# Splitting the load of token blocks 12 to 15 in two, and moving one output store on SyncE's queue, in a one-core attention-plus-MLP kernel

## The chip, the core and the metric

The kernel runs on one core of one Trainium2 chip. A core has five instruction streams that run side by side and wait for one another through semaphores: TensorE (PE, the matrix products, with its weight loads PEld), VectorE (DVE), ScalarE (ACT), GpSimd (POOL) and SyncE (SP), which here does nothing but issue DMA transfers. Each stream is worked off strictly in order. The metric is device time in microseconds of one launch.

## The reference

A token stream of 2048 x 640 (bfloat16) passes a pre-norm attention block with a compressive memory, and then a pre-norm MLP with SiLU. The sequence is cut into four segments of 512 tokens:

```python
for s in range(4):                                  # 32 heads of width 20
    qs, ks, vs = q[:, :, s], k[:, :, s], v[:, :, s]
    p = softmax(qs @ ks.T * 20 ** -0.5 + causal_mask)
    a_dot = p @ vs
    pq = phi(qs)                                    # phi(t) = t + 1 if t > 0 else exp(t)
    a_mem = (pq @ M) / (pq @ z + 1e-6)              # memory of the segments before
    outs.append(g * a_mem + (1 - g) * a_dot)        # g = sigmoid(beta)
    pk = phi(ks); M += pk.T @ vs; z += pk.sum(tokens)
h  = x + concat(outs) @ wo                          # q, k, v from layernorm(x)
h2 = h + silu(layernorm(h) @ w1) @ w2               # w1: 640 x 1728, w2: 1728 x 640
```

## The kernel before, in words

The 2048 tokens are 16 blocks of 128, four to a segment. All weights stay on the chip. The token blocks live in `x_tok`, a ring of 12 slots, so block 12 takes the slot of block 0, and so on to block 15 in the slot of block 3. A block is loaded, normalized, used as the residual of the attention output, normalized again, used as the residual of the MLP, and stored from the same slot.

Work is cut into tasks. The table `ORDER` lists all tasks in one hand-set order; each name goes to its engine's stream in the order of the table, and the number after a colon is a buffer slot. A tracker puts in the semaphore waits that the reads and writes need; DMA transfers have semaphores of their own, called lanes. So moving a name in `ORDER` moves an instruction in one engine's stream and changes what it stands behind. The names that matter here (the first digit is the segment, or the two digits the block):

- `x12` loads blocks 12 to 15 (L578, function `load_x`). Its slots are those of blocks 0 to 3, so it waits for the stores `out0` to `out3` (L1367), which share one lane, to land.
- `out0` stores output block 0 from `x_tok`; `o0` to `o3` (L1362, DVE) make the output blocks.
- `n1_st12` to `n1_st15` (L742, DVE) take the layer-norm statistics of the blocks of the last segment. On DVE they stand between steps `s1_...` of segment 1's MLP (L1322, writing `sT`), the first of them, `s1_1_0`, right behind `n1_st12`. A step `s1_f_0` also frees the PSUM bank in which the MLP product `h1_1_f_0` (L1307, PE) of that feature block stood, after `th1_f_0` (L1316, ACT) has read it.
- `vp1...` (L927, twelve small copies, function `pvirt`) copy pieces of `phiQ` into `phiQv`. A head is 20 wide and sits in 32 rows; the 12 spare rows of each hold pieces of further heads, the spare heads, and the copies bring their features to the front. Segment 1 has three memory products that read `phiQv`, and the first, in `tn13` (L1038, PE), waits for all twelve copies.
- `kt10`, `kt23` (L1207) are DMA transposes of key features; `n2_tr6`, `n2_tr7`, `n2_tr4`, `n2_tr5` (L798) are DMA transposes of the second layer norm's output of blocks 4 to 7 into `hT`, from a ring of four buffers `xn_rot`. The steps `n2_ap4` and `n2_ap5` (L769, DVE) write the two buffers that `n2_tr6` and `n2_tr7` have read, and so wait for these to land.

Of the kernel before, what the change touches and what calls it, by code (L numbers as in the profile page):

```python
# [324 lines left out]
D = 640  # L325
# [85 lines left out]
s0_1_1 qk18a0:2 e18a0:2 vt25/S av17:1 oe17/A:0 kt23:1 h2_2_0:6 h2_2_1 n2_ap6:1 n2_st5:6 n2_tr6:0 n2_r7/G mk18e_256
n2_ap7:3 n2_tr7 phb220 vt22/S e18a2 qk19b0:0 pha230:0 phb230 vp21/S:0 e19b0:4 tn17:4 nm17:3,1 n2_ap4:1 n2_tr4 pha200:0
h2_2_2 e19b2 h2_2_3 mk18a_0 n2_r5/G qk19a0:0 h2_3_0:4 h2_3_1 e19a2:0 o2 ad17:0 vp22/S e19a0 n2_ap5:3 n2_tr5 out2/S
mk19a_0 vp24/S ex200:0 kh14/D av18:6 oe18/D:0 vt210/A phb200 qk20b0:0 e20b+:3 h2_3_2 mk19b_0 h2_3_3 o3 vp25/S ex201:1
kg14/G mz12:7 mb10:0,0 tn18:1 nm18:3,0 mk19b_384 av19:0 h1_1_10_0:6 oe19/A:0 phb201 qk21b0:0 th1_10_0:1 tn16:4 ma12
# [40 lines left out]
h2_15_3_1 out15_0/A o15_1 h2_15_1_2 h2_15_2_2 h2_15_3_2 o15_2 out15_2/A out15_1/S fill2:2
""".split()


ONE_EXP = {row.partition("+")[0] for row in ORDER if row[0] == "e" and "+" in row}  # L460


def build(nc, es, A_x, A_wq, A_wk, A_wv, A_wo, A_beta, B_x, B_w1, B_w2, out):
    T = Tracker()
    pools = {
# [8 lines left out]
    G = Graph(pools)  # L474
# [950 lines left out]
```

## Time and profile before

| | |
|---|---|
| median of 3 runs | 298.25 us (298.09 to 298.98) |
| the profiled execution, its own time | 298.47 us |
| its span in the trace | 296.6 us |
| PE busy | 285.5 us |
| DVE, ACT, POOL busy | 222.1, 217.2, 140.0 us |
| granted TensorE clock | 1.0 |

The span runs from the first to the last instruction of the trace; the profiled execution's own time is 1.87 us more, for what lies around it. In rows of the trace the first number is the start in us from the span's beginning, the second the length, then the engine (SPq is SyncE's queue of DMA issues), the line, the operation, out<-in, a count, and in brackets how long the engine stood idle before it and who released it. A row for a DMA shows how long its issue took; when it landed is told by "DMA to landing", counted from the start of the issue. "issue" as the releaser means that the profile shows nothing that was waited for. A matmul row's end holds the time in which the last result drains, so the next row starts up to 0.2 us before that end.

### The profile page before, as it was taken

The page shows a single profiled execution, that of the slowest core. Times are in us where ns is not written, and L with a number is a line of the kernel's source. Part 1 is how long each engine was busy: PE and PEld are TensorE (multiplying, and loading weights), DVE is VectorE, ACT ScalarE, POOL GpSimd, SP SyncE. Part 2 cuts the span into 40 slices and gives each one's busy share as a digit, 9 for nine tenths or more (in the row PEclk, how much of TensorE's full clock was granted, in tenths as well). Part 3 has the DMA queues.
Part 4 walks back from the last instruction along what each step waited for, and adds up shares of the span by engine and source line. Part 5 has one row for each costly group of instructions (what it writes and reads, how often), then busy time and mean ns, then how long its engine had stood idle before and what let it go on. Part 6 is the DMA issues. An engine that isn't in the chain of part 4 may idle for free.

```text
span 296.6 us, 7437 instructions
## 1 busy us (share of the span) xinstructions
PE 285.5 (96%) x2991; PEld 168.3 (57%) x2991; DVE 222.1 (75%) x506; ACT 217.2 (73%) x266; POOL 140.0 (47%) x257
## 2 busy tenths in 40 slices
PE   8898889999999989999999999999999999999997
PEld 6775545545665445566643444465665457764575
DVE  3897899769979679899688967759967688626522
ACT  4985989999999888998879999788759751014400
POOL 6247836744655576646525656355576630200000
DMA  7958773804953321254452400144181023230002
GB/s 230 371 181 115 178 123 82 219 5 107 164 101 58 72 39 23 39 110 62 104 139 48 80 1 2 26 76 88 19 102 32 0 58 77 67 68 25 22 22 91
DMA packets 49906, 25.40 MB, mean 86 GB/s; under 512 B 39488, under 2 KB 48032, under 8 KB 49872
## 3 DMA queue, kind: packets, MB, share of 16 engines
q1 hardware_dynamic: 47788, 22.69, 36.5%
q10 hardware_dynamic: 2084, 2.23, 2.4%
q8 instruction: 24, 0.39, 0.6%
q14 instruction: 10, 0.08, 0.1%
HBM read 10.41 MB, written 2.62 MB: 44 GB/s over the span
## 4 chain that ended last, share of the span: by engine, by line
PE 80%; DVE 8%; DMA 4%; ACT 3%; POOL 2%; issue 2%; SPq 1%; DVEq 0%; ACTq 0%
PE ps_all L1349 19%; PE ps_all L1307 15%; PE ps_all L866 12%; PE ps_all L964 7%; PE ps_all L1272 7%; PE ps_all L827 5%; PE ps_all L1008 5%; ACT PT L976 2%; PE ps_all L619 2%; DMA x_tok<-in_A_x_dram 2%; PE ps_all L1092 2%; PE ps_all L1038 1%; PE ps_all L1225 1%; DMA w_sb<-w_sb 1%; POOL PT L987 1%
## 5 line engine op out<-in xcount | busy, mean ns | idle before, releaser
L976 ACT ACTIVATE PT<-ps_all 128x1024 bf16<-128x1024 f32 (+1 forms) x120 | 153.2, 1310 | 16.9 <-PE ps_all L964 15.7
L987 POOL TENSOR_SCALAR_AFFINE_SELECT PT<-PT 128x512 bf16<-128x512 bf16 x128 | 81.6, 648 | 59.6 <-ACT PT L976 57.5
L1349 PE MATMUL ps_all<-w_sb,sT 128*128 128x320 bf16 (+2 forms) x462 | 64.9, 295 | 0.0
L1307 PE MATMUL ps_all<-hT,w_sb 128*128 128x512 bf16 (+1 forms) x325 | 63.0, 337 | 0.6 <-DVE sT L1322 0.5
L1316 ACT ACTIVATE th<-ps_all 128x512 f32<-128x512 f32 (+2 forms) x70 | 34.1, 505 | 35.3 <-PE ps_all L1307 31.2
L1349 PEld LDWEIGHTS ps_all<-w_sb,sT 128*128 128x128 bf16 x462 | 43.2, 98 | 18.3 <-issue 1.8
L1322 DVE SCALAR_TENSOR_TENSOR sT<-th,ps_all 128x512 bf16<-128x512 f32 (+2 forms) x70 | 37.8, 560 | 16.9 <-ACT th L1316 16.0
L1307 PEld LDWEIGHTS ps_all<-hT,w_sb 128*128 128x128 bf16 x325 | 29.8, 98 | 26.0 <-issue 3.2
L763 POOL TENSOR_TENSOR rst<-rst,eps_c 128x1 f32<-128x1 f32 x32 | 18.3, 576 | 24.1 <-DVE rst L757 22.8
L742 DVE BATCH_NORM_STATS2 stt<-x_tok 128x6 f32<-128x320 bf16 x62 | 27.2, 481 | 2.6 <-DMA x_tok<-in_A_x_dram 2.2
L1362 DVE SCALAR_TENSOR_TENSOR x_tok<-ps_all,x_tok 128x640 bf16<-128x640 f32 (+3 forms) x18 | 13.3, 745 | 16.7 <-PE ps_all L1349 16.6
L1070 POOL TENSOR_TENSOR otok<-on 128x320 bf16<-128x320 bf16 x24 | 19.0, 797 | 11.4 <-DVE on L1062 11.4
L1272 PE MATMUL ps_all<-wo_sb,oT 128*128 128x320 bf16 x160 | 23.8, 299 | 0.0
L883 DVE CAST QK<-ps_all 128x512 bf16<-128x512 f32 x23 | 15.7, 688 | 8.8 <-PE ps_all L866 8.6
L1062 DVE TENSOR_TENSOR on<-ps_all,rd 128x640 bf16<-128x640 f32 x24 | 19.8, 825 | 0.9
L1272 PEld LDWEIGHTS ps_all<-wo_sb,oT 128*128 128x128 bf16 x160 | 15.0, 98 | 7.2 <-issue 1.8
L866 PE MATMUL ps_all<-xT,wkr 128*128 128x512 bf16 x75 | 18.7, 380 | 0.0
L827 PE MATMUL ps_all<-wv_sb,xT 128*128 128x320 bf16 x120 | 18.3, 299 | 0.3
L866 PE MATMUL ps_all<-xT,wqr 128*128 128x512 bf16 x75 | 18.2, 380 | 0.0
L1008 PE MATMUL ps_all<-PT,Vx 128*32 128x512 bf16 (+3 forms) x384 | 16.4, 301 | 0.1
L769 DVE TENSOR_SCALAR xn_rot<-x_tok,mvt,rst 128x640 bf16<-128x640 bf16 x32 | 15.0, 479 | 1.6 <-POOL rst L763 0.9
L842 DVE CAST Vx<-ps_all 128x640 bf16<-128x640 f32 x15 | 12.3, 818 | 5.2 <-PE ps_all L827 5.0
(106 smaller groups left out, 338.8 us busy)
## 6 DMA issues: line engine op xcount, KB each, us to landing
w_sb<-in_B_w_dram SPq DMA_DIRECT2D x5, 432.0 KB, 5.7
x_tok<-in_A_x_dram SPq DMA_DIRECT2D x3, 640.0 KB, 8.9
w_sb<-in_B_w_dram SPq DMA_DIRECT2D x3, 480.0 KB, 4.4
out_dram<-x_tok ACTq DMA_DIRECT2D x8, 160.0 KB, 1.8
out_dram<-x_tok SPq DMA_DIRECT2D x7, 160.0 KB, 2.0
QKV<-QK SPq DMA_DIRECT2D x12, 72.0 KB
wo_sb<-in_A_wo_dram SPq DMA_DIRECT2D x1, 800.0 KB, 10.0
w_sb<-in_B_w_dram SPq DMA_DIRECT2D x1, 640.0 KB, 4.3
```

What stands on the lines that cost most here:

```text
L742: T.add(DV, lambda e, hh=hh: e.bn_stats(out=stt[:, s, 6 * hh:6 * hh + 6], in_=xb[:, 320 * hh:320 * hh + 320]), reads=R((xa, xsub)), writes ...
L827: fns.append(lambda e, c=c, hh=hh: e.matmul(bank(ps, hh)[:, 0:320], lhsT=xT_[:, c, 128 * i:128 * i + 128], rhs=wv_sb[:, c, 320 * hh:320 * ...
L866: fns = [lambda e, kc=kc: e.matmul(bank(ps)[:, lo:hi], lhsT=wt[:, kc, c, :], rhs=xT_[:, kc, lo:hi], start=(kc == 0), stop=(kc == NC - 1)) ...
L964: fns.append(lambda e, j=j, o=o, r=r, q0=q0, q1=q1, qa=qa, ka=ka: e.matmul(ps_all[:, o:o + q1 - q0], lhsT=ka[32 * r:32 * r + DH, 128 * j:1 ...
L976: T.add(AC, lambda e: e.activation(out=pt[:, pta.slot, q0:q0 + nq, 0:width], in_=sc3[:, b0:b0 + nq, 0:width], func=ACT.Exp, scale=SCALE), ...
L987: T.add(PO, lambda e: e.affine_select(out=v, in_=v, pattern=[[0, 4], [1, 128]], compare_op=ALU.is_ge, fill=0.0, base=0, channel_multiplier ...
L1008: fns.append(lambda e, j=j, r=r, h=h, pa=pa, pt=pt, co=co, q0=q0, ji=ji: e.matmul(bank(po)[32 * r:32 * r + 32, q0:hi], lhsT=Vx[:, vx.slot, ...
L1272: fns.append(lambda e, c=c, hh=hh: e.matmul(bank(ps, hh)[:, 0:320], lhsT=oT[:, c, 128 * i:128 * i + 128], rhs=wo_sb[:, c, 320 * hh:320 * h ...
L1307: fns = [lambda e, c=c: e.matmul(bank(ps)[:, lo:hi], lhsT=w1_sb[:, c, 128 * f:128 * f + 128], rhs=hT[:, c, lo:hi], start=(c == 0), stop=(c ...
L1316: T.add(AC, lambda e: e.activation(out=th[:, tha.slot, lo:hi], in_=bank(ps)[:, lo:hi], func=ACT.Tanh, scale=0.5), reads=R((ps, [0])), writ ...
L1322: T.add(DV, lambda e: e.scalar_tensor_tensor(out=sT[:, f, lo:hi], in0=th[:, tha.slot, lo:hi], scalar=1.0, in1=bank(ps)[:, lo:hi], op0=ALU. ...
L1349: fns.append(lambda e, f=f, t0=t0, fr=fr, hh=hh, n=n: e.matmul(bank(pa, hh)[:, 0:n], lhsT=sT[:, f, t0:t0 + 128], rhs=w2_sb[:, fr, c0 + 320 ...
```

## The change

Two things move, and nothing that is computed changes.

1. The one load of blocks 12 to 15 (640 KB) becomes two of 320 KB, each with a lane of its own: `x12` for blocks 12 and 13 and `x14` for blocks 14 and 15. `x14` stands where `x12` stood, right behind `out3`. `x12` now stands much further ahead, behind the key transpose `kt23`, where of the lane of the stores only `out0` and `out1` are in front of it.
2. `out0` stood ahead of the transpose `kt10`, with seven of the twelve copies `vp1...` behind it; it now stands behind the last copy, `vp14`.

```diff
@@ ORDER
-ex231:2 tn11:6 nm11:0,1 pr200:4 qe200/A:0 mk12e_0 ex210:0 mk12e_256 qk14b0:0 av13:5 mzc7 oe13/D:1 out0/S mzc4 pha211:0
+ex231:2 tn11:6 nm11:0,1 pr200:4 qe200/A:0 mk12e_0 ex210:0 mk12e_256 qk14b0:0 av13:5 mzc7 oe13/D:1 mzc4 pha211:0
...
-th0_7_1:0 vp110/S vp12/S vp14/S tn13:6 nm13:2,1 ad13 pr201:5 qe201/A qk15a0:0 e15a2:4 e15a0 s0_7_1 tn10:6 nm10:2,0
+th0_7_1:0 vp110/S vp12/S vp14/S out0/S tn13:6 nm13:2,1 ad13 pr201:5 qe201/A qk15a0:0 e15a2:4 e15a0 s0_7_1 tn10:6
...
-s1_1_0 qk18a0:2 e18a0:2 vt25/S av17:1 oe17/A:0 kt23:1 h2_2_0:6 h2_2_1 n2_ap6:1 n2_st5:6 n2_tr6:0 n2_r7/G mk18e_256
+s0_1_1 qk18a0:2 e18a0:2 vt25/S av17:1 oe17/A:0 kt23:1 x12/S h2_2_0:6 h2_2_1 n2_ap6:1 n2_st5:6
...
-e20a+:2 out3/S x12/S n1_st12:6 n1_r12/G h1_1_1_0:4 th1_1_0:1 s1_1_0 vp210/S h1_1_12_0:7 th1_12_0:0 mk20b_0 n1_st13:0
+th1_7_0:1 th1_4_0:0 s1_7_0 s1_4_0 qk20a0:0 e20a+:2 out3/S x14/S n1_st12:6 n1_r12/G h1_1_1_0:4 th1_1_0:1 s1_1_0 vp210/S
...
@@ in build()
     for s in range(NSEG):
         if s == NSEG - 1:
-            load_x(12, 4, 8 * s + P["x3"])
+            load_x(12, 2, 8 * s + P["x3"])
+            load_x(14, 2, 8 * s + P["x3"])
         declare_front(s)
```

SyncE's queue around the copies of the spare heads' features, before: the row `out_dram<-x_tok` is `out0`, the `phiKt` row behind it `kt10`, the `phiQv` rows the copies, the two `hT` rows `n2_tr3` and `n2_tr2`.

```order
L927 DMA phiQv<-phiQ 12x1536
L1367 DMA out_dram<-x_tok 128x640
L1207 DMA_TRANSPOSE phiKt<-phiK 128x4x128
L927 DMA phiQv<-phiQ 8x1x512
L798 DMA_TRANSPOSE hT<-xn_rot 128x5x128
L927 DMA phiQv<-phiQ 8x1024
L798 DMA_TRANSPOSE hT<-xn_rot 128x5x128
L927 DMA phiQv<-phiQ 8x1024
L927 DMA phiQv<-phiQ 12x1536
L927 DMA phiQv<-phiQ 8x1024
L927 DMA phiQv<-phiQ 8x1x512
L927 DMA phiQv<-phiQ 8x1024
```

The same place in the changed kernel (all its lines below the table are one higher):

```order
L928 DMA phiQv<-phiQ 12x1536
L1208 DMA_TRANSPOSE phiKt<-phiK 128x4x128
L928 DMA phiQv<-phiQ 8x1x512
L799 DMA_TRANSPOSE hT<-xn_rot 128x5x128
L928 DMA phiQv<-phiQ 8x1024
L799 DMA_TRANSPOSE hT<-xn_rot 128x5x128
L928 DMA phiQv<-phiQ 8x1024
L928 DMA phiQv<-phiQ 12x1536
L928 DMA phiQv<-phiQ 8x1024
L928 DMA phiQv<-phiQ 8x1x512
L928 DMA phiQv<-phiQ 8x1024
L1368 DMA out_dram<-x_tok 128x640
```

Two transposes and seven copies that stood behind the store are now ahead of it.

SyncE's queue around the new place of `x12`, before: the `phiKt` row is `kt23`, the `hT` rows are `n2_tr6`, `n2_tr7`, `n2_tr4` and `n2_tr5`, the store is `out2`.

```order
L1207 DMA_TRANSPOSE phiKt<-phiK 128x4x128 [waits s_pool,s_dve]
L798 DMA_TRANSPOSE hT<-xn_rot 128x5x128 [waits s_pe,s_dve]
L798 DMA_TRANSPOSE hT<-xn_rot 128x5x128 [waits s_dve]
L914 DMA QKV<-QK 8x1x1024
L927 DMA phiQv<-phiQ 8x1024 [waits s_dve]
L798 DMA_TRANSPOSE hT<-xn_rot 128x5x128 [waits s_dve]
L927 DMA phiQv<-phiQ 8x1x512
L798 DMA_TRANSPOSE hT<-xn_rot 128x5x128 [waits s_dve]
L1367 DMA out_dram<-x_tok 128x640
```

And in the changed kernel:

```order
L1208 DMA_TRANSPOSE phiKt<-phiK 128x4x128 [waits s_pool,s_dve]
L579 DMA x_tok<-in_A_x_dram 128x2x640 [waits l_out0]
L799 DMA_TRANSPOSE hT<-xn_rot 128x5x128 [waits s_pe,s_dve]
L799 DMA_TRANSPOSE hT<-xn_rot 128x5x128 [waits s_dve]
L915 DMA QKV<-QK 8x1x1024
L928 DMA phiQv<-phiQ 8x1024 [waits s_dve]
L799 DMA_TRANSPOSE hT<-xn_rot 128x5x128 [waits s_dve]
L928 DMA phiQv<-phiQ 8x1x512
L799 DMA_TRANSPOSE hT<-xn_rot 128x5x128 [waits s_dve]
L1368 DMA out_dram<-x_tok 128x640
```

One more DMA, with a wait on the stores' lane, stands ahead of the four transposes. The streams of PE, ACT and POOL hold the same instructions in the same order as before; on DVE the only difference is a wait of `n1_st15` on the new lane of `x14`.

More of the change, by code (lines that the diff above doesn't have):

```diff
@@ L411 @@
[L411 to L415, printed above, removed]
@@ L456 @@
[L456 removed]
+th0_7_1:0 vp110/S vp12/S vp14/S out0/S tn13:6 nm13:2,1 ad13 pr201:5 qe201/A qk15a0:0 e15a2:4 e15a0 s0_7_1 tn10:6
+nm10:2,0 mk15a_0 pha201:2 pr221:5 av14:4 oe14/A:1 qe221/D av12:7 oe12/D:0 qk15b0:0 mb11:0,0 kg11/G tn14:4 nm14:1,1
+pr241:6 qe241/D:0 e15b+:0 mk15b_0 h1_0_12_1:7 th0_12_1:1 s0_12_1 kt14:0 vt26/S:0 ad14 mk15b_384 qk16b0:0 e16b0:2
+tn12:4 nm12:2,1 h1_0_4_1:6 th0_4_1:0 vt20/S s0_4_1 ad10 h1_0_10_1:7 e16b2 h1_0_0_1:0 th0_10_1:1 av15:1 ad12 th0_0_1:0
@@ new lines @@
+s0_0_1 s0_10_1 oe15/A:1 mk16b_0 mk16b_384 qk16a0:2 e16a2:4 h1_0_6_1:6 pha220:0 e16a0 tn15:0 nm15:1,0 pr240:7 qe240/D
+ex211:1 th0_6_1:1 s0_6_1 h1_0_5_1:4 ad15 th0_5_1:0 s0_5_1 qk16e0:0 mk16a_0 e16e0:5 ot6:0 ot7 e16e2 mk16e_0 pha210:0
+ot4 pr230:5 pha240:0 phb210 qe230/D v22:6 ve22/D ex230:0 ot5 out1/S h1_0_13_1:4 th0_13_1:0 qk17b0:0 e17b2:3
+h1_0_11_1:5 th0_11_1:1 vt29/S pha231:1 phb231 phb211 e17b0 wo6:6 mk16e_256 s0_13_1 s0_11_1 qk18b0:2 e18b2:6 mk17b_0
+e18b0 mk18b_0 rs6 n2_st6:3 ex220:2 av16:0 oe16/D:1 wo7:6 rs7 n2_r6/D qk17a0:2 wo4:0 vt28/S e17a+:0 h1_0_9_1:7
@@ new lines @@
+th0_9_1:0 ex240:1 kg10/G vt27/S n2_st7:0 mk18b_384 vt21/S mk17b_384 vt211/S h1_0_3_1:6 mk17a_0 rs4 th0_3_1:1 n2_st4:2
+s0_9_1 qk18e0:2 e18e0:1 n2_r4/D wo5:0 s0_3_1 vt23/S h1_0_2_1:7 e18e2 mk18e_0 phb240 rs5 th0_2_1:0 s0_2_1 h1_0_1_1:6
+th0_1_1:1 vt24/S s0_1_1 qk18a0:2 e18a0:2 vt25/S av17:1 oe17/A:0 kt23:1 x12/S h2_2_0:6 h2_2_1 n2_ap6:1 n2_st5:6
+n2_tr6:0 n2_r7/G mk18e_256 n2_ap7:3 n2_tr7 phb220 vt22/S e18a2 qk19b0:0 pha230:0 phb230 vp21/S:0 e19b0:4 tn17:4
+nm17:3,1 n2_ap4:1 n2_tr4 pha200:0 h2_2_2 e19b2 h2_2_3 mk18a_0 n2_r5/G qk19a0:0 h2_3_0:4 h2_3_1 e19a2:0 o2 ad17:0
@@ new lines @@
+vp22/S e19a0 n2_ap5:3 n2_tr5 out2/S mk19a_0 vp24/S ex200:0 kh14/D av18:6 oe18/D:0 vt210/A phb200 qk20b0:0 e20b+:3
+h2_3_2 mk19b_0 h2_3_3 o3 vp25/S ex201:1 kg14/G mz12:7 mb10:0,0 tn18:1 nm18:3,0 mk19b_384 av19:0 h1_1_10_0:6 oe19/A:0
+phb201 qk21b0:0 th1_10_0:1 tn16:4 ma12 s1_10_0:0 nm16:0,1 e21b+:4 mk21b_0 mk21b_384 h1_1_7_0:7 h1_1_4_0:6 ad18
+th1_7_0:1 th1_4_0:0 s1_7_0 s1_4_0 qk20a0:0 e20a+:2 out3/S x14/S n1_st12:6 n1_r12/G h1_1_1_0:4 th1_1_0:1 s1_1_0 vp210/S
+h1_1_12_0:7 th1_12_0:0 mk20b_0 n1_st13:0 n1_r13/G mk20b_384 vp28/S qk20e0:0 h1_1_11_0:5 n1_ap12:3 e20e+:0 h1_1_8_0:4
@@ new lines @@
+qk21a0:0 s1_12_0 th1_11_0:1 h1_1_5_0:6 e21a+:5 th1_5_0:0 n1_st15:5 mk21a_0 n1_ap13:2 mk20a_0 s1_11_0 s1_5_0 mk20e_0
+mk20e_256 h1_1_2_0:7 th1_2_0:1 s1_2_0 vp20/S qk22a0:0 e22a0:6 kt20:0 vp211/S kg20/G:0 n1_st14:4 vp26/S th1_8_0:1
+kg23/D n1_r14/D h1_1_6_0:5 th1_6_0:0 vp29/S n1_tr12:0 v30:6 n1_r15/D s1_6_0 e22a2 h1_1_0_0:0 n1_ap14:0 s1_8_0
+n1_ap15:3 mk22a_0 kh23/G av21:1 ve30/A:1 mb12:0,0,0,0 av20:2 qk22b0:3 vp23/S th1_0_0:0 s1_0_0 n1_tr13 mz20:7 ma20
+oe21/A:1 e22b+:1 mk22b_0 vp27/S tn21:0 h1_1_9_0:7 th1_9_0:1 ad16 nm21:1,0 n1_tr14 qk23a0:3 oe20/D:1 e23a+:0 s1_9_0
@@ new lines @@
+e24a+:5 pr340:0 pr331:1 qe331/A qe340/D vt310/S vt32/S tn22:2 mk24b_384 qk26b0:4 nm22:3,0 e26b+:1 ad22 ot11:0
+mk24e_256 v31:0 ve31/D phb221 mk24a_0 kg21/D kt22:1 vt35/A ot9 pha300:0 h1_1_13_0:2 qk25b0:3 th1_13_0:1 s1_13_0
+pha340:0 vt37/S h2_4_0:0 h2_4_1 e25b0:6 e25b2 h2_4_2 mk25b_0 mk25b_384 qk26a0:2 e26a2:4 h2_4_3 o4 vt34/S kg22/G av25:7
+e26a0 mk26a_0 av24:5 vt31/S oe25/A:1 oe24/D:0 pha310:0 phb310 ex300:2 qk26e0:0 phb300 wo11:6 vt38/S e26e+:5 mk26b_0
+vt36/S ex340:0 rs11 wo9:4 n2_st11:5 rs9 ex320:2 qk27b0:0 e27b0:2 h2_5_0:6 e27b2 n2_r11/D phb330 mz21:1 ma21 vt33/S
@@ new lines @@
+e29a2:6 e29a0 phb320 qk30e0:2 e30e2:1 vp38/S n2_ap9:0 mk28b_384 n2_tr9 o6 n2_ap8:2 n2_tr8 e30e0 tn26:0 nm26:2,0
+mk30e_0 vp37/S ad26 h2_7_3 o7 vp39/A h1_2_7_0:5 th2_7_0:0 s2_7_0:0 qk30a0:0 e30a0:4 h1_2_13_0:7 th2_13_0:0 av28:4
+oe28/D:1 mk30e_256 vp311/S h1_2_4_0:6 mb22:0,0,0,0 tn28:4 s2_13_0 e30a2 mk30a_0 th2_4_0:1 s2_4_0 nm28:3,0 mk29b_384
+qk30b0:0 e30b+:0 h1_2_0_0:7 th2_0_0:1 vp36/S vp33/S h1_2_1_0:6 qk31b0:0 th2_1_0:0 s2_1_0 e31b2:3 mk29a_0 h1_2_6_0:4
+mk30b_0 vp310/S s2_0_0 e31b0 av29:5 mk30b_384 av30:6 ad27 mk31b_0 qk31a0:0 e31a0:0 th2_6_0:1 h1_2_12_0:7 vp31/S
@@ new lines @@
+mk31b_384 e31a2 mk31a_0 oe29/D:1 oe30/D:0 vp30/S vp34/S tn30:5 nm30:3,1 ad30 h1_2_3_0:0 th2_3_0:0 h1_2_10_0:1 s2_3_0
+tn29:2 av31:5 oe31/A:0 s2_6_0 nm29:3,1 h1_2_9_0:6 ad28 tn31:4 nm31:3,0 th2_12_0:0 ad29 h1_2_2_0:0 h1_2_11_0:2
+h1_2_5_0:3 ad31 ot12:0 th2_2_0:1 out6/A s2_12_0 s2_2_0 th2_10_0:0 h2_9_0:4 s2_10_0 h1_2_8_0:7 th2_11_0:1 th2_5_0:0
+h2_8_0:0 s2_5_0 th2_9_0:0 s2_11_0 th2_8_0:1 s2_8_0 out4/A wo12:2 ot14 h2_8_1 s2_9_0 wo14:6 rs12 n2_st12:5 rs14
+n2_r12/D n2_st14:1 ot13 wo13:2 rs13 n2_st13:0 ot15 n2_r13/G wo15:6 n2_r14/D rs15 n2_st15:4 h2_8_2 h2_8_3 h2_9_1 o8
@@ L457 @@
+h2_13_1 h1_3_10_0:0 th3_8_0:0 s3_8_0 h2_13_2 h2_14_0:1 th3_10_0:1 s3_10_0 h2_14_1 h2_13_3 h2_14_2 o13 out13/A h2_12_1
+h2_14_3 o14 out14/S h2_12_2 h2_12_3 o12 h2_15_0_0:4 h2_15_1_0 h2_15_2_0 h2_15_3_0 o15_0 out12/A out9/A h2_15_0_1:6
+h2_15_1_1 h2_15_2_1 h2_15_0_2:3 h2_15_3_1 out15_0/A o15_1 h2_15_1_2 h2_15_2_2 h2_15_3_2 o15_2 out15_2/A out15_1/S
+fill2:2
 """.split()
```

64 lines of the change are left out of this document (15 added, 49 removed).

## The prediction

> **What bounds the kernel now.** I read the page first, then PE's list of waits, then the chain of waits and the timelines of the two places that the change touches.
>
> ```profile
> span 296.6 us, 7437 instructions
> PE 285.5 (96%) x2991; PEld 168.3 (57%) x2991; DVE 222.1 (75%) x506; ACT 217.2 (73%) x266; POOL 140.0 (47%) x257
> PE 80%; DVE 8%; DMA 4%; ACT 3%; POOL 2%; issue 2%; SPq 1%; DVEq 0%; ACTq 0%
> ```
>
> PE is busy for 96% of the span and carries 80% of the chain. The other engines only matter where they make PE wait, and there is little of that: 296.6 - 285.5 = 11.1 us in all. So the question is which of PE's gaps the change can close. Two entries of PE's waits lie at the two places:
>
> ```profile
> PE ps_all L1038 <- issue: 0.8, 1, 0.8
> PE ps_all L1307 <- DVE sT L1322: 0.5, 1, 0.5
> ```
>
> The columns are us in total, times and the longest. These two, 0.8 and 0.5 us, are all that a perfect version of the change could take from PE directly. The second hangs on the load, as the chain of waits shows (start, length, what):
>
> ```profile
> 148.98 1.77 DMA out_dram<-x_tok
> 150.77 5.79 DMA x_tok<-in_A_x_dram
> 156.57 0.90 DVE stt L742 x2
> 157.71 0.56 DVE sT L1322
> 158.31 1.25 PE ps_all L1307 x5
> ```
>
> Store out3, then the load x12, then the statistics, then one MLP step on DVE, then PE. The DMA stretch is 7.6 us long in the chain, but that isn't what it costs: PE had other work until just before 158.31.
>
> **The store out0, moved.** SyncE's queue around it, and what PE does at tn13:
>
> ```profile
> 96.98 0.52 SPq L1367 DMA_DIRECT2D out_dram<-x_tok  x1
> 97.55 2.90 SPq L1207 DMA_TRANSPOSE phiKt<-phiK  x1
> 104.89 3.51 SPq L927 DMA_DIRECT2D phiQv<-phiQ  x5
> 115.45 1.20 SPq L1207 DMA_TRANSPOSE phiKt<-phiK  x1
> 104.62 0.90 POOL L1249 TENSOR_TENSOR Mzb<-Mz,MzM 128x336 bf16<-128x336 f32 x1
> 105.80 0.75 DVE L1023 TENSOR_SCALAR oTs<-ps_all,lsc 128x512 bf16<-128x512 f32 x1 [0.35 <-PE ps_all L1008]
> 109.84 0.31 PE L1038 MATMUL ps_all<-Mzb,phiQv 128*128 128x84 bf16 x4 [0.80 <-issue]
> L1207 SPq DMA_TRANSPOSE phiKt<-phiK x15: 1198/1258/2895, 26.3 to 204.1; - x15
> q8 instruction: 1, 0.02, 21.3%
> ```
>
> The last copy's issue ends at 104.89 + 3.51 = 108.40, and tn13 starts 1.44 us later. What else it reads was written long before, the memory by 104.62 + 0.90 = 105.52 and the attention output oTs by 105.80 + 0.75 = 106.55, so the 0.80 us, for which the view names nobody, are the wait for these copies to land. Between 97.55 and 108.40 the queue is full nearly end to end. Taking out0 from ahead of kt10 brings everything behind it forward by 97.55 - 96.98 = 0.57 us. There may be more: kt10's issue took 2.90 us where the median of these transposes is 1.26 (ns in the row: smallest, median, largest). In the half microsecond from 97.5 to 98, the last row, the instruction queue moved one packet that kept an engine of the 16 busy for 21.3% of 16 x 0.5, so 1.7 us. (Its columns are packets, MB and the share of the 16 engines.) My reading is that the store's rows on that engine waited for the packet, and kt10 for them. Without the store, kt10 may take its usual 1.26, and the copies gain 0.57 + 1.64 = 2.2 us.
>
> So the bounds for the copies are 0 (kt10's end is held by the instruction packet at its own time, rival below) and 2.2 us; for PE 0 and 0.80, since 2.2 is more than the gap. With 0.57 alone 0.23 of the gap is left. I take 0.80, since 1.26 is the median of 15 such transposes. Out0 itself goes into a free stretch: after 108.40 the queue issues nothing until kt11 at 115.45, so its 0.52 us hide there; without that pause kt11 would be 0.57 us later. Only x12 waits for its landing, some 25 us later.
>
> Do the 0.80 us stay? The engines around it:
>
> ```profile
> 108.45 1.88 ACT L976 ACTIVATE PT<-ps_all 128x2048 bf16<-128x2048 f32 x1
> 111.42 0.60 ACT L882 ACTIVATE QK<-ps_all 128x512 bf16<-128x512 f32 x1 [0.82 <-PE ps_all L866]
> 110.14 1.25 PE L866 MATMUL ps_all<-xT,wkr 128*128 128x512 bf16 x5
> ```
>
> ACT waited 0.82 us for PE right behind the gap, so it can follow. The next scores need the banks that ACT's exponential frees at 108.45 + 1.88 = 110.33; PE would reach them at 110.14 + 1.25 - 0.80 = 110.6. So the 0.8 us are kept.
>
> **The load, split and begun early.** The place where it is waited for now:
>
> ```profile
> 156.57 0.89 DVE L742 BATCH_NORM_STATS2 stt<-x_tok 128x6 f32<-128x320 bf16 x2 [1.48 <-DMA x_tok<-in_A_x_dram]
> 156.03 1.09 ACT L1316 ACTIVATE th<-ps_all 128x512 f32<-128x512 f32 x2
> 156.60 1.25 PE L1307 MATMUL ps_all<-hT,w_sb 128*128 128x512 bf16 x5
> 158.31 1.25 PE L1307 MATMUL ps_all<-hT,w_sb 128*128 128x512 bf16 x5 [0.46 <-DVE sT L1322]
> 159.95 1.88 ACT L976 ACTIVATE PT<-ps_all 128x2048 bf16<-128x2048 f32 x1 [0.56 <-PE ps_all L964]
> 160.12 0.88 DVE L742 BATCH_NORM_STATS2 stt<-x_tok 128x6 f32<-128x320 bf16 x2
> 160.00:165.00 5.00, 4.89 (x29) 2.20 (x28) 4.74 (x15) 5.00 (x7) 3.67 (x8) 1.00 0.39 76
> ```
>
> With blocks 12 and 13 there long before, DVE's 1.48 us are gone: statistics at 155.09 instead of 156.57. The step s1_1_0 behind them then waits for its th, the first of ACT's two from 156.03, so for about 156.6, and is done near 157.3, before PE ends its products at 156.60 + 1.25 = 157.85. PE's gap of 0.46 closes. ACT, which waited 0.56 us for PE at 159.95, follows by about as much, and no more: from 160 to 165 ACT is busy 5.00 of 5.00 us (the fourth engine of the window's row), so the rest of DVE's 1.48 us has nobody to give it to. Bounds: 0, if ACT sets this stretch anyway, and 1.48, if every engine moved up with DVE. I take 0.5, between PE's 0.46 and ACT's 0.56. Blocks 14 and 15 are wanted at 160.12 now (block 15's statistics), at about 158.6 after the change. Their load is issued where x12 was; even if the half took the full 5.79 us from 150.77, it would be there at 156.56, and the wait is 0.
>
> What the early half costs: one issue more, and transposes behind it.
>
> ```profile
> 128.97 0.59 SPq L1367 DMA_DIRECT2D out_dram<-x_tok  x1
> 135.66 1.21 SPq L1207 DMA_TRANSPOSE phiKt<-phiK  x1
> 138.37 2.55 SPq L798 DMA_TRANSPOSE hT<-xn_rot  x2
> DMA to landing us min/median/max: 2.6/3.5/4.3
> 142.26 0.44 DVE L769 TENSOR_SCALAR xn_rot<-x_tok,mvt,rst 128x640 bf16<-128x640 bf16 x1
> 144.16 0.45 DVE L769 TENSOR_SCALAR xn_rot<-x_tok,mvt,rst 128x640 bf16<-128x640 bf16 x1
> 145.80 0.75 DVE L1023 TENSOR_SCALAR oTs<-ps_all,lsc 128x512 bf16<-128x512 f32 x1 [1.05 <-PE ps_all L1008]
> 144.81 1.20 SPq L798 DMA_TRANSPOSE hT<-xn_rot  x1
> 149.59 1.25 PE L1307 MATMUL ps_all<-hT,w_sb 128*128 128x512 bf16 x5
> 153.54 1.23 SPq L1207 DMA_TRANSPOSE phiKt<-phiK  x1
> DMA to landing us min/median/max: 3.4/3.4/3.4
> ```
>
> Out1 was issued at 128.97, so x12's wait on it is over by then; kt23's issue ends at 136.87 and the next transposes start at 138.37, held by DVE. The issue of x12 fits into these 1.5 us if it takes no longer than the store's 0.59, and even a landing 5.79 us after it is 12 us ahead of the statistics. Behind it, in the same queue, n2_tr6 and n2_tr7 landed 2.6 and 4.3 us after their issue (the smallest and the largest of the first landing row, which is theirs), so at 140.97 and near 143.96. DVE waits for them to reuse their buffers: n2_ap4 started at 142.26, n2_ap5 at 144.16. So a delay d of both costs DVE nothing up to 1.3 us at the first and all of it at the second, and there 1.05 us of idle time follow before 145.80. PE is touched only when n2_tr5 (issue at 144.81, with n2_tr6's 2.6 us at 147.4) comes after 149.59: that is 2.2 us of cover. The nearest rows for d are the last two: the transpose kt20, issued at 153.54 behind the whole load, landed after 3.4 us where n2_tr6 took 2.6, so 0.8. The bounds are 0 and, if the transposes waited out a load of the full length, 5.79. I take 0.8, and PE's cost as 0.
>
> The Trainium skill, "DMA: Bandwidth & Descriptors", section "Bandwidth", speaks against the split: it asks to batch transfers to 1 MiB or more, and gives 6.15 us for 1 MB against 0.95 us for 64 KB. Drawn straight between these, an estimate is 4.1 us for 640 KB and 2.3 for each half, so 0.6 us more of transfer; by that rule, counted on the path, the gain below would be 0.7. No run here shows a half load; the second half has 158.6 - 150.77 = 7.8 us by the rows, so I don't count it.
>
> **Sum.** 298.47 - 0.80 - 0.50 = 297.17 against the profiled execution's own time; that lies 0.22 above the median of the runs, 298.25, so 296.95, or 297.0.
>
> **Rivals.**
>
> Only the load counts: kt10's issue ends when the instruction packet lets it, at 100.45 with or without the store ahead. For it: the packet comes at its own time, and keeps its engine until 97.5 + 1.7 = 99.2 at least. Against it: n2_tr7 in the row above landed late (4.3) and still its issue took no longer (2.55 for two). The gain is then 0.5: 297.75. Chance 0.15.
>
> Only the store counts: ACT's full stretch after 159.95 eats what PE gains before it. Against it is ACT's own wait of 0.56 for PE. The gain is 0.8: 297.45. Chance 0.10.
>
> More than forecast: DVE's whole 1.48 us pass on, because its backlog held PE in other places up to 165 (PE 4.89 of 5.00). 298.25 - 0.80 - 1.48 = 295.97. Against it: ACT at 5.00. Chance 0.09.
>
> Slower: the early half holds up the transposes. Place: n2_tr6, n2_tr7 behind x12, then n2_ap5, then n2_tr5, then PE at 149.59. PE loses d - 2.2; against the gain of 1.3 the kernel gets slower from d = 3.5. At the upper bound, 5.79, PE loses 3.6: 298.25 - 1.3 + 3.6 = 300.55. Against it: kt20's 0.8. Chance 0.07. The Trainium skill has a rule on this side, in the same page, section "Queues, rings and completion order": each DMA engine takes its descriptors in ring order, so the transposes do stand behind the load's rows; kt20's 3.4 us agrees.
>
> **How the numbers follow.** The forecast, both gaps closed, has 0.59 and by itself a range from 296.6 (0.3 more at the knock-on of ACT and DVE) to 297.4 (0.23 left of the first gap, and 0.2 of spread between runs). A measurement of this kernel can tell about 0.3% from no change, 0.9 us: faster is below 297.35, slower above 299.15. Faster: nearly all of the forecast, 0.52 of 0.59, the larger gain, 0.09, and a little of the store alone, 0.01, so 0.62. Same: 0.30, the load alone, 0.15, most of the store alone, 0.08, and 0.07 of the forecast. Slower: 0.08, the last rival and 0.01 for what I don't see. The range for 8 in 10 leaves out the slower rival and most of the larger gain, and takes in the load alone: 296.3 to 298.0.
>
> **What would show it.** Right: PE's list has no wait of L1038 for "issue" and none of L1307 for sT at these places; out0 stands in the pause after the copies; kt10's issue takes 1.2 to 1.3 us; the statistics wait for no DMA; PE reaches the scores after each place 0.8 and then 1.3 us earlier than before. Wrong: kt10 still at 2.9 us with its end near 100.4; a new wait of L769 for hT above 1 us, or of L1307 for a DMA near 149; or both gaps closed and a stretch of the same length where PE waits for ACT between 159 and 172.

## The result, and the profile after

The changed kernel takes 297.0 us in the median of 20 runs (296.56 to 298.95), the kernel before, beside it, 298.48 (20 runs, 297.29 to 299.67). The ratio is 0.9955, with a 95% interval of 0.994 to 0.9969: faster by 0.3% to 0.6%, about 1.3 us. The profiled execution took 298.11 us, only 0.36 us less than the profiled one of before, because it lost time in two other places, mostly at its start; where, is told below. Its span is 296.3 us. The page of the changed kernel:

```profile
span 296.3 us, 7415 instructions
PE 282.1 (95%) x2968; PEld 167.6 (57%) x2991; DVE 222.2 (75%) x506; ACT 217.3 (73%) x266; POOL 140.0 (47%) x257
```

PE's busy time looks 3.4 us smaller, but the row counts 2968 matmuls where the program has 2991: 23 records are missing, and the busy time can't be compared. The other engines' busy times are as they were. So the place to look is the timeline. SyncE's queue and PE at the copies, after (start, length, what):

```profile
97.83 2.02 SPq L1208 DMA_TRANSPOSE phiKt<-phiK  x1
104.29 3.52 SPq L928 DMA_DIRECT2D phiQv<-phiQ  x5
107.86 0.44 SPq L1368 DMA_DIRECT2D out_dram<-x_tok  x1
109.16 0.72 PE L1308 MATMUL ps_all<-hT,w_sb 128*128 128x256 bf16 x5
109.72 0.31 PE L1039 MATMUL ps_all<-Mzb,phiQv 128*128 128x84 bf16 x4
```

The store stands behind the copies (kt10, n2_tr3 and n2_tr2 are now ahead of it too: three transposes, not the two that the text on the change counts), kt10's issue takes 2.02 us instead of 2.90, and tn13 follows PE's row before it with no idle time (it starts 0.16 us before that row's end, which is the drain). The same PE row of before, and three later ones, to lay beside the after rows:

```profile
108.33 0.72 PE L1307 MATMUL ps_all<-hT,w_sb 128*128 128x256 bf16 x5
159.82 2.33 PE L1307 MATMUL ps_all<-hT,w_sb 128*128 128x512 bf16 x10
170.25 1.53 PE L827 MATMUL ps_all<-wv_sb,xT 128*128 128x320 bf16 x10
171.62 1.24 PE L866 MATMUL ps_all<-xT,wkr 128*128 128x512 bf16 x5
```

Ahead of tn13 the changed execution is 109.16 - 108.33 = 0.83 us late, behind it 109.72 - 109.84 = -0.12: 0.95 us were gained there. The 0.83 come from the first 44 us, where nothing was changed. About 0.5 of them are there by 35 us; the rest comes with this row:

```profile
42.68 1.53 PE L828 MATMUL ps_all<-wv_sb,xT 128*128 128x320 bf16 x10 [0.85 <-DMA xT<-xn_rot]
```

This wait for a transposed block isn't in the profile of before, where PE instead waits 0.48 us for ACT a row later; five of the eight later profiles have it, with 0.4 to 1.6 us, the store alone and the late split among them.

The place of the load, after:

```profile
136.81 0.68 SPq L579 DMA_DIRECT2D x_tok<-in_A_x_dram  x1
138.25 2.55 SPq L799 DMA_TRANSPOSE hT<-xn_rot  x2
DMA to landing us min/median/max: 3.2/3.6/4.1
142.14 0.44 DVE L770 TENSOR_SCALAR xn_rot<-x_tok,mvt,rst 128x640 bf16<-128x640 bf16 x1
154.90 0.88 DVE L743 BATCH_NORM_STATS2 stt<-x_tok 128x6 f32<-128x320 bf16 x2
156.55 0.69 DVE L1323 SCALAR_TENSOR_TENSOR sT<-th,ps_all 128x512 bf16<-128x512 f32 x1 [0.53 <-ACT th L1317]
156.70 2.11 PE L1308 MATMUL ps_all<-hT,w_sb 128*128 128x512 bf16 x9 [0.16 <-issue]
159.16 2.33 PE L1308 MATMUL ps_all<-hT,w_sb 128*128 128x512 bf16 x10
159.28 1.88 ACT L977 ACTIVATE PT<-ps_all 128x2048 bf16<-128x2048 f32 x1
```

The statistics wait for no DMA, the two products of the MLP follow one another (the small wait for "issue" at 156.70 stands where a matmul record is missing), and the row of 159.82 now starts at 159.16, 0.66 us earlier: 0.54 gained beyond the 0.12. The early half cost nothing: its two followers, n2_tr6 and n2_tr7, landed 3.2 and 4.1 us after their issue (the landing row is of these two) where they took 2.6 and 4.3, and the first write behind them on DVE starts at 142.14, 0.12 us earlier than before, as PE does.

Then a part is given back:

```profile
169.58 1.53 PE L828 MATMUL ps_all<-wv_sb,xT 128*128 128x320 bf16 x10
171.25 1.24 PE L867 MATMUL ps_all<-xT,wkr 128*128 128x512 bf16 x5
DMA to landing us min/median/max: 2.6/3.6/4.6
```

The first row is 0.67 us earlier than in the profile of before, the second, `pr301` of the last segment, only 0.37. It reads block 15's transpose n1_tr15, the second of a pair issued at 165.33, whose landings are the last row. The second was issued at 166.6 and landed 4.6 us later, at 171.2. From there to the end the offset stays -0.37. Net of its start, the profiled execution gained 0.83 + 0.37 = 1.20 us, which is 0.95 + 0.54 less the 0.30 given back, to a hundredth.

### The profile page after: what moved, and what is told of

It reads as the page before. It is cut to its first block, busy times and chain, and to the rows that moved or that the text cites. A ratio compares the mean times of both kernels' runs of the same rounds, so it can differ in the third digit from the quotient of the medians.

```text
span 296.3 us, 7415 instructions
## 1 busy us (share of the span) xinstructions
PE 282.1 (95%) x2968; PEld 167.6 (57%) x2991; DVE 222.2 (75%) x506; ACT 217.3 (73%) x266; POOL 140.0 (47%) x257
## 4 chain that ended last, share of the span: by engine, by line
PE 78%; DVE 8%; DMA 6%; issue 2%; ACT 2%; SPq 1%; POOL 1%; DVEq 0%; ACTq 0%
PE ps_all L1350 19%; PE ps_all L1308 17%; PE ps_all L867 12%; PE ps_all L965 7%; PE ps_all L1273 6%; PE ps_all L828 5%; PE ps_all L1009 5%; DMA x_tok<-in_A_x_dram 3%; DMA xT<-xn_rot 2%; ACT PT L977 2%; PE ps_all L1039 1%; DVE stt L743 1%; PE ps_all L1093 1%; DMA w_sb<-w_sb 1%; PE ps_all L1226 1%
## 5 line engine op out<-in xcount | busy, mean ns | idle before, releaser
L1308 PE MATMUL ps_all<-hT,w_sb 128*128 128x512 bf16 (+1 forms) x315 | 61.0, 336 | 1.2 <-issue 0.6
L867 PE MATMUL ps_all<-xT,wkr 128*128 128x512 bf16 x67 | 16.9, 379 | 1.2 <-issue 0.8
L867 PE MATMUL ps_all<-xT,wqr 128*128 128x512 bf16 x70 | 17.3, 380 | 0.4 <-issue 0.2
```

The source lines that it names most:

```text
L867: fns = [lambda e, kc=kc: e.matmul(bank(ps)[:, lo:hi], lhsT=wt[:, kc, c, :], rhs=xT_[:, kc, lo:hi], start=(kc == 0), stop=(kc == NC - 1)) ...
L1308: fns = [lambda e, c=c: e.matmul(bank(ps)[:, lo:hi], lhsT=w1_sb[:, c, 128 * f:128 * f + 128], rhs=hT[:, c, lo:hi], start=(c == 0), stop=(c ...
```

## The experiments

Eight kernels ran, in two groups of four; the median of the kernel before was 298.07 us beside both groups (35 and 32 runs). The first group takes the change apart.

**The store alone.** The two edits on `out0`, nothing else:

```diff
-... oe13/D:1 out0/S mzc4 ...
+... oe13/D:1 mzc4 ...
-... vp110/S vp12/S vp14/S tn13:6 ...
+... vp110/S vp12/S vp14/S out0/S tn13:6 ...
```

> Only the store out0 is moved; the load stays one, at its old place. Theory that the two parts add, each closing its own gap of PE: no idle time of PE ahead of tn13, PE there 0.8 to 0.95 us earlier against the products just before it, the statistics of block 12 still wait about 1.5 us for the load, total 0.8 to 1.0 us less than before. Rival that the parts are not separate (the store alone brings nothing, because the instruction packet holds kt10 and the copies): PE still stands about 0.8 us at tn13, total as before. Rival that the store is all of the gain: total 1.3 us less.

Measured: 297.84 us (12 runs), ratio 0.9995 (0.9975 to 1.0014). That can't be told from no change (0.23 us less by the medians, where 0.8 to 1.0 was expected), so the trace has to speak. This kernel's timeline at both places:

```profile
98.70 2.10 SPq L1207 DMA_TRANSPOSE phiKt<-phiK  x1
105.23 3.52 SPq L927 DMA_DIRECT2D phiQv<-phiQ  x5
109.65 0.72 PE L1307 MATMUL ps_all<-hT,w_sb 128*128 128x256 bf16 x5
110.21 0.31 PE L1038 MATMUL ps_all<-Mzb,phiQv 128*128 128x84 bf16 x4
157.40 0.89 DVE L742 BATCH_NORM_STATS2 stt<-x_tok 128x6 f32<-128x320 bf16 x2 [1.94 <-DMA x_tok<-in_A_x_dram]
159.14 1.25 PE L1307 MATMUL ps_all<-hT,w_sb 128*128 128x512 bf16 x5 [0.92 <-DVE sT L1322]
```

The first gap is gone, but only just: tn13 starts 110.21 - (105.23 + 3.52) = 1.46 us after the copies' last issue, where the profile of before, which waits for them, has 1.44. The second, untouched here, is 0.92 us where it was 0.46, because the whole load landed after 6.2 us instead of 5.8: what the load costs varies by the execution.

**The load alone.** The edits on `x12` and `x14`, with `out0` at its old place:

```diff
-            load_x(12, 4, 8 * s + P["x3"])
+            load_x(12, 2, 8 * s + P["x3"])
+            load_x(14, 2, 8 * s + P["x3"])
-... kt23:1 h2_2_0:6 ...
+... kt23:1 x12/S h2_2_0:6 ...
-... out3/S x12/S n1_st12:6 ...
+... out3/S x14/S n1_st12:6 ...
```

> Only the load is split and its first half begun ahead; out0 stays ahead of kt10. Theory that the two parts add: PE stands about 0.8 us at tn13 as before; DVE does not wait for the load, PE's gap of 0.46 us behind the step s1_1_0 is gone, and up to 0.3 us of it are given back at the first key projection of the last segment, where PE now waits for the transpose n1_tr15; total 0.2 to 0.55 us less than before. Rival that ACT, busy throughout behind that place, eats it all: 0 to 0.1 us less.

Measured: 297.76 us (12 runs), ratio 0.9994 (0.9971 to 1.0017).

```profile
100.11 2.28 SPq L1207 DMA_TRANSPOSE phiKt<-phiK  x1
106.81 3.51 SPq L927 DMA_DIRECT2D phiQv<-phiQ  x5
110.84 0.72 PE L1307 MATMUL ps_all<-hT,w_sb 128*128 128x256 bf16 x5
111.76 0.31 PE L1038 MATMUL ps_all<-Mzb,phiQv 128*128 128x84 bf16 x4 [0.20 <-issue]
156.93 0.88 DVE L742 BATCH_NORM_STATS2 stt<-x_tok 128x6 f32<-128x320 bf16 x2
158.51 2.33 PE L1307 MATMUL ps_all<-hT,w_sb 128*128 128x512 bf16 x10
```

The load's gap is gone (ten products in one row, no wait of the statistics). But at tn13, where this kernel is the kernel before, the gap is 0.20 us and not 0.80: here kt10's issue took 2.28. The 1.44 us from the copies' last issue to tn13 are the same: 111.76 - (106.81 + 3.51) = 1.44. Nothing was given back at pr301: n1_tr15 landed after 4.2 us here.

**Split, but not early.** As the one before, with both halves issued at the old place of the load (`out3/S x12/S x14/S`).

> The load is split, but both halves are issued right behind out3, where the one load stood; out0 stays ahead of kt10. Theory that size alone is enough (a half landed in 3.4 and 3.1 us in the changed kernel): blocks 12 and 13 land near 154.3, before DVE wants them at about 155.0, so DVE waits at most 0.2 us and the total is that of the kernel with the load alone split and begun ahead, 0.2 to 0.55 us less than before. Rival that the early start is what counts (the two halves share the engines and land together, 5.8 us after the issue): DVE waits 1.3 us or more and the total is that of before.

Measured: 297.54 us (12 runs), ratio 0.9975 (0.9963 to 0.9988).

```profile
98.18 1.90 SPq L1207 DMA_TRANSPOSE phiKt<-phiK  x1
104.54 3.51 SPq L927 DMA_DIRECT2D phiQv<-phiQ  x5
108.72 0.72 PE L1307 MATMUL ps_all<-hT,w_sb 128*128 128x256 bf16 x5
109.49 0.31 PE L1038 MATMUL ps_all<-Mzb,phiQv 128*128 128x84 bf16 x4
154.65 0.88 DVE L742 BATCH_NORM_STATS2 stt<-x_tok 128x6 f32<-128x320 bf16 x2
```

The view of the load's line gives the issues (shortest, median, longest in ns, then the first and the last start) and their landings:

```profile
L578 SPq DMA_DIRECT2D x_tok<-in_A_x_dram x2: 408/440/471, 150.4 to 150.9; - x2
DMA to landing us min/median/max: 3.2/4.2/5.2
```

Two things follow. The load's gap is gone without the early begin (PE's rows have no wait there): the first half landed 3.2 us after its issue, at 150.4 + 3.2 = 153.6, a microsecond ahead of the statistics. And at tn13 the gap is nearly gone too, with the store still at its old place: 0.05 us lie between the PE row's end at 109.44 and tn13, which still waits for the copies, 109.49 - (104.54 + 3.51) = 1.44. kt10 took 1.90 us here. So the 0.80 us of the profile of before don't belong to the order of the queue alone.

**The changed kernel once more**, word for word.

> The changed kernel once more, on the chip of the three before it. If the two parts add, its gain is the sum of the gains of the store alone and of the load alone, within 0.3 us: 1.1 to 1.5 us less than before. If they overlap, it is no better than the better of the two.

Measured: 297.27 us (12 runs), ratio 0.9982 (0.9967 to 0.9997). By the medians that is 0.80 us less, under the 1.1 to 1.5 expected. The two parts alone have 0.23 and 0.31, together 0.54, so the times agree with adding within 0.3 us, but the intervals of the parts are wider than that and decide nothing. In the trace, neither gap is there. The wait of `pr301` isn't either: n1_tr15 landed after 4.3 us here.

The second group was made for what the first left open: how far the gap at tn13 varies, and what holds kt10.

**The kernel before once more**, word for word.

> The kernel before, unchanged, to see how far its two gaps vary from execution to execution. Theory: the instruction packet falls just behind the start of kt10 in every execution, and its length varies (1.70 us in the first profile of this kernel; 0.99 and 1.20 in the two experiments that also had the store at its old place), so kt10's issue takes between 1.9 and 2.9 us, ends about 1.05 us after the packet, and TensorE's gap ahead of tn13 lies between 0 and 0.8 us. The whole load lands 5.8 to 6.2 us after its issue, and TensorE's gap ahead of h1_1_8 is 0.46 to 0.92 us. Rival: the gap of 0.80 us belongs to the order of the queue, and this profile shows 0.7 to 0.9 again. Ratio to the other runs of the kernel before: 1.000 within 0.002.

Measured: 298.26 us (12 runs), ratio 1.0004 (0.999 to 1.0019); this also shows what no change looks like.

```profile
97.31 2.44 SPq L1207 DMA_TRANSPOSE phiKt<-phiK  x1
107.85 0.72 PE L1307 MATMUL ps_all<-hT,w_sb 128*128 128x256 bf16 x5
109.15 0.31 PE L1038 MATMUL ps_all<-Mzb,phiQv 128*128 128x84 bf16 x4 [0.58 <-issue]
155.84 0.89 DVE L742 BATCH_NORM_STATS2 stt<-x_tok 128x6 f32<-128x320 bf16 x2 [1.43 <-DMA x_tok<-in_A_x_dram]
157.57 1.25 PE L1307 MATMUL ps_all<-hT,w_sb 128*128 128x512 bf16 x5 [0.42 <-DVE sT L1322]
```

The gap at tn13 is 0.58, between the theory's bounds and under the rival's 0.7. The packet began at 97.24, just ahead of kt10's issue and not behind its start, as had been expected. The load's landing, 5.7 us, and PE's gap behind it, 0.42, lie just under the ranges expected.

**The store past kt10 only.** It tells whether the store's data hold kt10, or only its 0.57 us of issue:

```diff
-... oe13/D:1 out0/S mzc4 ...
+... oe13/D:1 mzc4 ...
-... kt10:1 e14b+:5 ...
+... kt10:1 out0/S e14b+:5 ...
```

> Only the store out0 is moved, and only past kt10: it stands between kt10 and the next copy, vp111. Theory (the store's rows on the packet's engine hold kt10): kt10's issue ends 0.4 to 0.5 us after the end of the instruction packet, as in the three runs with the store behind the copies, and not about 1.05 as in the three with the store ahead of it; the copies still start 0.5 us later for the store's own issue. Rival (the packet alone holds kt10, and the store costs only its own 0.57 us of issue): kt10 ends about 1.05 us after the packet here too.

Measured: 298.21 us (12 runs), ratio 1.0003 (0.999 to 1.0016).

```profile
97.08 2.64 SPq L1207 DMA_TRANSPOSE phiKt<-phiK  x1
99.76 0.59 SPq L1367 DMA_DIRECT2D out_dram<-x_tok  x1
104.78 3.52 SPq L927 DMA_DIRECT2D phiQv<-phiQ  x5
108.39 0.72 PE L1307 MATMUL ps_all<-hT,w_sb 128*128 128x256 bf16 x5
109.75 0.31 PE L1038 MATMUL ps_all<-Mzb,phiQv 128*128 128x84 bf16 x4 [0.64 <-issue]
```

kt10 takes 2.64 us with no store ahead of it, so the packet alone stretches it. To see how far, the instruction queue's row was read in windows of 0.02 us, in which a packet counts where it begins. For the kernel before, from 97.66:

```profile
q8 instruction: 1, 0.02, 531.6%
```

The share times 16 engines times 0.02 us is the time that the packet kept its engine: 531.6% gives 1.70 us. All ten profiles, worked out in this way (times in us), are in the table. Its last column tells how late the copies are for tn13. It is the end of their last issue, plus the 1.44 us that pass from there to tn13 wherever tn13 waits (1.44 or 1.45 in five profiles), less the time at which tn13 could start without a gap, 0.16 us before the end of the PE row ahead of it. A minus means time to spare, and is an estimate, since tn13 doesn't wait there.

| | store | packet begins | its length | kt10's issue ends | behind the packet's end | copies late at tn13 |
|---|---|---|---|---|---|---|
| before | ahead of kt10 | 97.66 | 1.70 | 100.45 | 1.09 | 0.95 |
| load alone | ahead | 100.12 | 1.19 | 102.39 | 1.08 | 0.36 |
| split late | ahead | 98.08 | 0.99 | 100.08 | 1.01 | 0.21 |
| before again | ahead | 97.24 | 1.43 | 99.75 | 1.08 | 0.74 |
| after | behind the copies | 98.50 | 0.94 | 99.85 | 0.41 | -0.47 |
| store alone | behind the copies | 99.02 | 1.34 | 100.80 | 0.44 | -0.02 |
| after again | behind the copies | 98.76 | 1.30 | 100.48 | 0.42 | -0.07 |
| both, split late | behind the copies | 97.32 | 1.18 | 98.93 | 0.43 | -0.25 |
| block 15 early | behind the copies | 98.06 | 1.22 | 99.71 | 0.43 | -0.17 |
| store past kt10 | just behind kt10 | 97.74 | 1.56 | 99.72 | 0.42 | 0.80 |

The column behind the packet's end has two values and nothing between: kt10's issue ends 1.01 to 1.09 us behind the packet where the store is ahead of it, and 0.41 to 0.44 where it isn't. The rival expected 1.05 in the last line and falls. So kt10 waits for the packet in all ten, and the store ahead of it adds about 0.65 us. And since the store between kt10 and the copies still holds up the copies by its own 0.63 us (100.39 - 99.76, from its start to the next copy's), that kernel won nothing.

The store's own 0.57 us of issue ahead of kt10 is no gain on top. The packet doesn't come with the queue: in all ten profiles it begins 10.61 to 10.72 us before the PE row ahead of tn13 (for before, 108.33 - 97.66 = 10.67). Without the store ahead kt10 starts sooner, 11.0 to 11.3 us before that row where it was 10.5 to 10.8, and waits longer for the same packet. Behind kt10's end the rest is fixed: 7.93 to 7.97 us to the end of the last copy's issue, 8.58 with the store between. So two things set how late the copies are, the packet's length and the place of the store. The last column is the length less 0.69 to 0.83 us with the store ahead of kt10, less 0.76 just behind kt10, and less 1.36 to 1.43 behind the copies. On average the move is worth 1.39 - 0.76 = 0.63 us.

**Both, with the split late.** The store moved as in the change, both halves at the old place of the load.

> The store moved as in the change, the load split, but both halves issued at the late place, one behind the other. Theory: the first half lands 3.2 us after its issue, in time for the statistics, so this does all that the change does: no gap of TensorE at tn13 nor at h1_1_8, and a time equal to the changed kernel's, 297.0 to 297.5 us, 0.7 to 1.3 below the kernel before. Rival: the early begin is needed; then DVE waits for the first half and TensorE keeps 0.2 us or more of its gap at h1_1_8.

Measured: 297.17 us (9 runs), ratio 0.9967 (0.9948 to 0.9987).

```profile
108.01 0.72 PE L1307 MATMUL ps_all<-hT,w_sb 128*128 128x256 bf16 x5
108.57 0.31 PE L1038 MATMUL ps_all<-Mzb,phiQv 128*128 128x84 bf16 x4
DMA to landing us min/median/max: 3.0/3.9/4.8
153.74 0.88 DVE L742 BATCH_NORM_STATS2 stt<-x_tok 128x6 f32<-128x320 bf16 x2
```

No gap at either place, and a time that can't be told from the changed kernel's beside it in the other group. The early begin isn't needed.

**Block 15's normalization earlier**, on top of the change; one step of it, `n1_r15`, goes from DVE to GpSimd with it (`/D` to `/G`):

```diff
-... n1_st15:5 mk21a_0 n1_ap13:2 mk20a_0 s1_11_0 s1_5_0 mk20e_0
+... n1_st15:5 n1_r15/G mk21a_0 n1_ap13:2 mk20a_0 s1_11_0 n1_ap15:1 s1_5_0 mk20e_0
...
-... n1_tr12:0 v30:6 n1_r15/D s1_6_0 ...
+... n1_tr12:0 v30:6 s1_6_0 ...
-n1_ap15:3 mk22a_0 kh23/G ...
+mk22a_0 kh23/G ...
-... nm21:1,0 n1_tr14 qk23a0:3 ...
+... nm21:1,0 n1_tr15 n1_tr14 qk23a0:3 ...
-v32:0 ve32/D n1_tr15 pr301:2 ...
+v32:0 ve32/D pr301:2 ...
```

> The changed kernel, and the normalization of block 15 (n1_r15, n1_ap15, n1_tr15) earlier by some steps, since in one profile of the changed kernel the first values-and-keys product pr301 waited 0.30 us for n1_tr15, whose landing took 4.6 us. Theory: that wait is gone, and the time is 0 to 0.3 us below the changed kernel's, so 0.7 to 1.5 below the kernel before. Rival: the landing of 4.6 us was a chance of that execution (4.2 to 4.3 in the other five profiles, none with the wait), and this brings nothing, or costs some tenths on DVE.

Measured: 297.1 us (12 runs), ratio 0.9971 (0.9956 to 0.9985).

```profile
DMA to landing us min/median/max: 2.6/2.6/2.6
162.92 1.52 PE L828 MATMUL ps_all<-wv_sb,xT 128*128 128x320 bf16 x10 [0.38 <-DVE sT L1323]
```

The four transposes of these blocks now all land after 2.6 us, but DVE's step is later by the normalization put ahead of it, and PE waits 0.38 us for that. It is a trade, no gain that can be measured.

## Why the prediction was right

The forecast of 297.0 us was met by the median of the first 20 runs, and both gaps closed, as it said. For the load the working holds. For the store only the direction does: two terms of its sum were wrong, and that the whole gap closed in the first pair of profiles was in part luck. The steps:

- **The store term, 0.80.** Right that the gap closes: it is gone in all five profiles with the store behind the copies. Its size was that of one execution. By the table, the copies were 0.95 us late in the profile of before, and 0.36, 0.21 and 0.74 in the other three with the store at its old place, 0.57 in the mean. The prediction took its price from a single profile, and that one had the longest packet of the ten. The profile after had the shortest, 0.94 against 1.70. An estimate from the table: with a packet of 1.70 the copies of the changed kernel would still be 1.70 - 1.39 = 0.31 us late. So of the 0.95 us gained there about 0.64 are the move's, and the rest is the packet's. With the store behind the copies no packet longer than 1.34 was seen, and that one left 0.02 us to spare. Whether the move also shortens the packet can't be told: its mean is 1.33 in the four profiles with the store at its old place and 1.20 in the five with it behind the copies, and the two overlap.
- **The copies' gain, 0.57 + 1.64 = 2.2.** Wrong in both terms. kt10's issue took 2.02 and not 1.2 to 1.3 (1.90 to 2.90 over all ten): the step "Without the store, kt10 may take its usual 1.26" failed. And the 0.57 us of the store's issue never reached the copies, because kt10 then waits that much longer for the packet. The rival that the instruction packet sets kt10's end was right in that, and wrong only in "with or without the store": the store adds 0.65 us. So the copies gained about 0.65 us and not 2.2, less than the 0.95 wanted, and the short packet hid the error.
- **The load term, 0.5.** Right in size: 0.54 in the profiled pair. It varies too: PE's gap was 0.46, 0.92, 0.42 and 0.33 us in the four profiles with the whole load (the last is that of the store past kt10). DVE's whole 1.48 us did not pass on, and ACT did follow by the 0.67 us of 159.95 - 159.28, of which 0.12 were there already: 0.55.
- **The early half.** The cost of 0 was right, and d smaller than taken: 0.6 us at n2_tr6, less than nothing at n2_tr7. But the prediction never asked whether the early begin was needed. Both kernels with the late split show that it isn't: halving brings the first half's landing to 3.0 and 3.2 us where the whole took 5.7 to 6.2, and 1.48 us were wanted.
- **The Trainium skill's rule to batch transfers** ("DMA: Bandwidth & Descriptors", section "Bandwidth"), weighed against the split at 0.6 us more of transfer, an estimate from the page's figures for loads issued from GpSimd. The runs, whose loads SyncE issues, show no such cost: with the halves issued back to back, the second landed at 150.9 + 5.2 = 156.1, so 5.7 us after the first issue (5.2 in the kernel with both, split late: 149.9 + 4.8 - 149.5), where the whole took 5.7 to 6.2.
- **Not foreseen:** the 0.30 us given back at pr301. It isn't the change's own: n1_tr15 landed after 4.2 to 4.3 us in seven of the ten profiles, the changed kernel's second among them, none of which has the wait, and after 4.6 in the first profile after; the kernel before, run again, had 4.5 and lost 0.21 us at this place against its first profile: 171.09 - 169.51 between the two PE rows, where that had 171.62 - 170.25.

How much the change brings in the mean is less sure than that it brings something. Two comparisons of it gave 0.9955 and 0.9982, whose intervals only just touch, so 1.3 and 0.5 us. From the traces, the store brings 0.57 us less what long packets would leave, 0.31 and 0.04 us in two of the four by the estimate above, so about 0.5, and the load the mean of the four gaps, (0.46 + 0.92 + 0.42 + 0.33) / 4 = 0.53: about 1.0 us. By time the parts don't separate: the store alone has 0.9995, the load alone 0.9994, the late split alone 0.9975 and the whole change beside them 0.9982. That both parts count is shown by the traces, not by those ratios.

## What to carry to other kernels

A gap that hangs on a DMA's issue or landing has a size only over several executions: one profile gives the mechanism, and here a gap of 0.80 us was 0.05 to 0.80 in four profiles of the same order. Before counting on what a shorter queue brings, ask what its next member waits for: kt10, started sooner, waited longer for the packet. Move a large store off the stretch of a queue in which small copies are awaited, and move it past all of them, worth 0.63 us here: past the transpose alone, still ahead of the copies, won nothing. Where a consumer needs only the first part of a load, split the load before looking for an earlier place for it; the split alone closed the gap here.

## What the hardware showed that was not expected

An instruction packet of 0.02 MB kept its DMA engine for 0.94 to 1.70 us, at the same place of the program in ten executions (10.61 to 10.72 us before the same PE row, whatever stood in SyncE's queue), and SyncE's issue of the transpose then under way ended a fixed time after it: 0.41 to 0.44 us, or 1.01 to 1.09 with a 160 KB store queued ahead. My reading is that the store's rows on that engine have to pass between the packet and the transpose; that it is these rows, and not the store as a whole, was not tried. Nor was it found whose instructions the packet carries, so that it could be moved.
